# Last batch's C loaded in three parts, experts that pause behind each eviction, another order behind the loop

## The chip, the cores and the metric

One core of a Trainium2 chip runs the program. The metric is the device time of one execution in microseconds. TensorE is called PE here, VectorE DVE, ScalarE ACT, GpSimd POOL, and SyncE, which here only issues transfers, SP.

## What is computed

Eight batches of 3136 x 256 numbers go through a Fourier transform along the 3136 positions, a complex 256 x 256 weight with a soft threshold, and the inverse transform. Then, in each batch, the 128 positions with the highest score go through one expert (256 to 1024, ReLU, 1024 to 256), whose result is added with a sigmoid gate.

```python
X = np.fft.rfft(x, axis=1)
Yr = Xr @ w_r - Xi @ w_i + b_r
Yi = Xr @ w_i + Xi @ w_r + b_i
Yr = np.sign(Yr) * np.maximum(np.abs(Yr) - lam, 0.0)    # Yi likewise
y = np.fft.irfft(Y, n=x.shape[1], axis=1)
...
scores = np.einsum('bsd,d->bs', x, w_gate)
for b in range(B):
    top_idx = np.argpartition(-scores[b], capacity)[:capacity]
    xe = x[b, top_idx]
    ye = np.maximum(xe @ w1, 0.0) @ w2
    out[b, top_idx] = x[b, top_idx] + g[:, None] * ye   # g: sigmoid of the score
```

## The kernel before

**Stages.** The transform is factored as 98 x 32. Forward stage 1 (`s1`, lines 398 to 415) multiplies folded input by `w` and stores the result as `As` in DRAM. Forward stage 2 (`s2`, L441) reads `As` in units, 13 or 12 of them in each batch (the thirteenth of every second batch holds the odd rows of two batches). `spectral` (L223 to L225) multiplies a unit by the weights, `shrink` (L479, L481) thresholds it, `s2i` (L502) is inverse stage 2 and puts its result as `C` into DRAM (`Cs`), four units to a store (L525); it also reduces the score of each position on DVE (L514, `Csc`). `ld_c` reads C back in four blocks of 8 columns by 98 rows to a batch, 784 KB each; `s1i` (L570) is inverse stage 1 in eight pieces to a batch, and every second piece makes a group of three stores to the output.

**Experts.** `route` picks the positions of a batch: `score`, then `select`, which counts in eight rounds how many scores reach a threshold (one product, L243, and a string of DVE operations each; called a count below), then `place`, which makes the index `idx` (L326). `fetch` gathers the rows by an indirect transfer from POOL's queue (`xe`, L332). `ffn` takes an expert through `prepare` (transposes, L343, copy `xT`, L346, gate `ga` on ACT, L352), `hidden` (two halves of four pieces, L361, each half evicted with a ReLU to `hh`, L366) and `combine` (eight pieces, L372; `ye`, L377; scatter, L378). These are generators: each `yield` gives the turn back, and a `tick` runs them on to their next one.

**The order.** It is written out by hand: engines run what the program issues in the order in which it is issued. T = 100 steps, one per unit, each of which issues stage 2 of the next unit, the products of its own, inverse stage 2 of the unit before, and between them a piece or two of `s1` or `s1i`, the turns of `route`, and two or three ticks of the experts. SP's queue takes all large transfers in that order. `bank` names the PSUM bank of an expert's results; in the loop it is one bank, `m`, so the next results wait until the last are evicted.

**Behind the loop** a second loop goes on with t = T, T + 1, ... It issues the last unit's inverse stage 2, loads C of batch 7 (`rest` holds its eight pieces; `ready` says from which t a piece may be issued), and shares PE out between counts of batch 7, pieces of `s1i` and ticks of the experts, by an estimate of PE's time in `load`; `idle` issues products without use.

```python
    def ready():
        b, i = rest[0]
        return b < B - 1 or t > T + 4 + 3 * (i // 2) // 2
...
        for k in range(4):
            if t >= T and len(rest) <= (16, 16, 10, 8)[k] and (B - 1, k) not in cv:
                ld_c(B - 1, 2 * k)
                ld_c(B - 1, 2 * k + 1)
```

## Time and profile before

| | us |
|---|---|
| median of 3 runs | 728.84 (727.83 to 730.57) |
| the profiled execution | 729.37 |
| its span | 727.5 |
| PE busy | 650.9 (89%) |
| DVE busy | 443.8 (61%) |
| ACT busy | 364.6 (50%) |
| POOL busy | 293.5 (40%) |

The page gives these shares over the whole span. In the loop, from about 46 to 664 us, a step lasts between some 4.5 and 9 us, and PE's share is nine tenths or more in nearly every slice. Behind the loop the slices thin out. For the stretches between, the timeline of each engine, its list of waits and the chain that ended last are read: a wait in square brackets is the time that the engine sat idle before the row, and the releaser is what ended it.

### The profile page before, as it was taken

The numbers are of one execution on the slowest core, as the hardware profiler recorded it, in microseconds if no ns is written. First come the engines' busy times: TensorE is split into PE (matmuls) and PEld (weight loads), VectorE is DVE, ScalarE is ACT, GpSimd is POOL, SyncE is SP. The second block draws the span as 40 slices with busy tenths as digits, with TensorE's granted clock in tenths as the row PEclk, the third lists the DMA queues.
The fourth block names the chain that finished last, engine by engine and source line by source line (L and its number), as shares of the span: only waits on it lengthen the run. The fifth ranks groups of instructions, "written<-read, shape, count | busy, mean of one in ns | idle before, by whom it ended". The sixth has DMA issues, their size and how long they took to land.

```text
span 727.5 us, 20428 instructions
## 1 busy us (share of the span) xinstructions
PE 650.9 (89%) x8333; PEld 479.8 (66%) x8333; DVE 443.8 (61%) x1393; ACT 364.6 (50%) x671; POOL 293.5 (40%) x247
## 2 busy tenths in 40 slices
PE   2769989999999999999999999899999999987865
PEld 0247767767776677766777777676777777665535
DVE  4516566777677666656477566765676567773520
ACT  1326546466655565544555456555654555543230
POOL 4148565545445445345444445444542122221001
PEclk9869999999999999999999999999999999999996
DMA  8979976899989998979569778979785755754570
GB/s 150 277 233 318 264 205 166 221 300 263 276 259 272 308 292 236 312 217 269 177 166 296 216 220 223 326 228 249 224 256 158 208 161 156 235 169 113 189 171 23
DMA packets 79198, 163.73 MB, mean 225 GB/s; under 512 B 5918, under 2 KB 58496, under 8 KB 72832
## 3 DMA queue, kind: packets, MB, share of 16 engines
q1 hardware_dynamic: 77920, 160.15, 77.3%
q0 software_dynamic: 896, 2.17, 1.0%
q8 instruction: 66, 1.08, 0.6%
q14 instruction: 28, 0.23, 0.1%
q10 hardware_dynamic: 288, 0.10, 0.1%
HBM read 84.35 MB, written 78.12 MB: 223 GB/s over the span
## 4 chain that ended last, share of the span: by engine, by line
PE 59%; DVE 14%; DMA 12%; issue 6%; ACT 6%; POOL 2%; SPq 1%; POOLq 0%; DVEq 0%; ACTq 0%
PE pca L502 9%; PE s L570 6%; PE px L441 5%; DVE junk L514 5%; PE py L223 5%; PE py L225 4%; PE py L224 4%; PE s L407 4%; PE pcb L223 4%; PE m L361 3%; PE m L372 3%; DVE Xl L454 2%; ACT ct L512 2%; PE pcb L225 2%; PE pcb L224 2%
## 5 line engine op out<-in xcount | busy, mean ns | idle before, releaser
L470 POOL TENSOR_TENSOR kb<-ks,bias 128x512 f32<-128x512 f32 x100 | 127.9, 1279 | 323.6 <-ACT ks L468 322.0
L396 POOL TENSOR_TENSOR sd<-xt 113x512 f32<-113x512 f32 x106 | 133.8, 1284 | 28.4 <-DMA xt<-in_x 20.3
L512 ACT COPY ct<-pcb 128x256 f32<-128x256 f32 (+1 forms) x100 | 37.3, 373 | 170.5 <-PE pcb L502 159.8
L474 DVE TENSOR_TENSOR py<-py,kb 128x512 f32<-128x512 f32 x100 | 69.9, 699 | 78.9 <-POOL kb L470 73.9
L454 DVE TENSOR_TENSOR Xl<-px,Xh 128x768 fp32r<-128x768 f32 x100 | 95.6, 956 | 19.3 <-ACT Xh L453 19.3
L502 PE MATMUL pca<-Y,gi_sb 64*64 64x256 f32 x760 | 101.8, 386 | 5.8 <-DVE pca L240 5.5
L502 PE MATMUL pcb<-Y,gi_sb 64*64 64x256 f32 x768 | 103.3, 386 | 0.0
L514 DVE CUSTOM_DVE_ANT_0 junk<-pcb,wgb 128x256 f32<-128x256 f32 (+1 forms) x100 | 42.4, 424 | 98.9 <-ACT ct L512 97.4
L441 PEld LDWEIGHTS px<-g_sb,av 64*64 64x64 f32 x3072 | 78.9, 135 | 19.2 <-issue 5.7
L453 ACT CAST Xh<-px 128x768 fp32r<-128x768 f32 x100 | 81.0, 810 | 17.0 <-PE px L441 15.3
L441 PE MATMUL px<-g_sb,av 64*64 64x96 f32 x3072 | 84.3, 246 | 5.5 <-DMA av<-As 5.3
L407 PE MATMUL s<-sd,w 49*64 49x512 f32 x480 | 72.7, 638 | 12.9 <-DVE sd L396 10.7
L572 ACT COPY ot<-s 128x1024 f32<-128x1024 f32 x58 | 60.1, 1036 | 44.8 <-PE s L570 44.8
L479 ACT ACTIVATE r<-py,m2l 128x512 f32<-128x512 f32 x100 | 70.3, 703 | 8.2 <-DVE py L474 7.9
L502 PEld LDWEIGHTS pca<-Y,gi_sb 64*64 64x64 f32 x760 | 46.5, 132 | 41.9 <-issue 11.3
L409 ACT COPY at<-s 128x1024 f32<-128x1024 f32 x58 | 60.7, 1046 | 18.9 <-PE s L407 18.9
L481 DVE SCALAR_TENSOR_TENSOR Y<-py,r 128x512 f32<-128x512 f32 x100 | 68.5, 685 | 1.6 <-ACT r L479 1.6
L223 PE MATMUL pcb<-wsh,Xh 128*128 128x256 f32 x200 | 65.7, 328 | 1.2 <-DVE Csc L514 1.2
L570 PE MATMUL s<-cv,wi_sb 64*64 64x512 f32 x464 | 62.6, 599 | 0.0
L223 PE MATMUL py<-wnh,Xh 128*128 128x256 f32 x200 | 56.8, 284 | 1.3 <-DVE Y L481 1.2
L225 PE MATMUL pcb<-wsl,Xh 128*128 128x256 f32 x200 | 56.3, 281 | 0.0
L224 PE MATMUL pcb<-wsh,Xl 128*128 128x256 f32 x200 | 56.2, 281 | 0.0
(169 smaller groups left out, 1358.6 us busy)
## 6 DMA issues: line engine op xcount, KB each, us to landing
Cs<-ct SPq DMA_DIRECT2D x48, 512.0 KB
av<-As SPq DMA_DIRECT2D x46, 512.0 KB
As<-at SPq DMA_DIRECT2D x30, 784.0 KB
cv<-Cs SPq DMA_DIRECT2D x30, 784.0 KB
out<-ot SPq DMA_DIRECT2D x60, 384.0 KB
xt<-in_x SPq DMA_DIRECT2D x56, 384.0 KB
cv<-in_x SPq DMA_DIRECT2D x8, 384.0 KB
As<-ot SPq DMA_DIRECT2D x2, 784.0 KB
```

The lines of the kernel that those rows point to most:

```text
L223: nc.tensor.matmul(out, wh, mh, start=start, stop=False)
L224: nc.tensor.matmul(out, wl, mh, start=False, stop=False)
L225: return nc.tensor.matmul(out, wh, ml, start=False, stop=stop).ins
L396: eng.tensor_tensor(out=f[:113, k], in0=t[:113, 0], in1=t[:113, 1], op=op)
L407: nc.tensor.matmul(p[64 * c:64 * c + 64, r, :], w[64 * r:64 * r + NH, c, :], f[64 * r:64 * r + NH, c], start=True, stop=True)
L441: nc.tensor.matmul(o[:, :, N2 * j:N2 * j + N2], a[64 * p:64 * p + 64, j, g % 4, 128 * h + 64 * q:128 * h + 64 * q + 64], g_sb[64 * p:64 * ...
L453: nc.scalar.copy(out=vh, in_=v)
L454: nc.vector.tensor_tensor(out=vl, in0=v, in1=vh.bitcast(F32), op=ALU.subtract)
L470: nc.gpsimd.tensor_tensor(out=kb[:r], in0=ks[:r].broadcast_to([r, 2, D]), in1=bias[:r], op=ALU.add)
L502: nc.tensor.matmul(p[q][64 * a:64 * a + 64], gi_sb[64 * q:64 * q + 64, g, c, 64 * a:64 * a + 64], y[64 * q:64 * q + 64, c, :], start=(c == ...
L514: nc.vector.tensor_tensor_reduce(out=junk[:r], in0=p[k][:r], in1=wgb[:r], scale=1.0, scalar=0.0, op0=ALU.mult, op1=ALU.add, accum_out=Csc[ ...
L570: nc.tensor.matmul(p[64 * c:64 * c + 64, r, :], wi_sb[64 * r:64 + NH * r], f[64 * r:64 + NH * r, 4 * c + 2 * e:4 * c + 2 * e + 2, :], star ...
```

## The change

- C of batch 7 is loaded by `ld_last` instead of `ld_c`. Of each block, rows 0 to 31 and row 48 of both halves (66 of 98 rows) are the early part, rows 32 to 47 (32 rows) the late one. The early parts of blocks 0 and 1 are issued in step T - 2, that of block 2 in step T - 1, that of block 3 and the four late parts behind the last unit's store.
- `prepare` and each half of `hidden` are followed by `pause`, which gives turns back until the next step has begun, as long as the loop runs. The ReLU is issued right behind its half's last product, no longer with the next product.
- Behind the loop `ready` lets a piece of batch 7's `s1i` go from t > T + 2 + i // 2; the work in t = T is smaller (1.2, experts alone); batch 6's expert starts six steps behind its gather instead of three; eight idle products instead of six stand ahead of batch 7's expert.
- Batch 0's thirteenth unit and batch 1's first change places in the list of units.

```diff
--- before.py
+++ after.py
@@ -352,27 +352,37 @@
         nc.scalar.activation(out=ga, in_=sg, func=AF.Sigmoid)
         return xT, ga
 
+    def pause():
+        t = done["t"]
+        while done["t"] == t:
+            yield
+
     def hidden(b, k, xT, hs):
         n = min(128, cap - 128 * k)
         for q in range(FF // 512):
             ph = ps.tile([128, 4, n], F32, name=bank(b, 1 + q % 2), bufs=1)
             for f in range(4):
+                if f > 0:
+                    yield
                 for h in range(2):
                     nc.tensor.matmul(ph[:, f, :], w1s[:, h, (4 * q + f) * 128:(4 * q + f + 1) * 128], xT[:, h, :],
                                      start=(h == 0), stop=(h == 1))
                 load[0] += 0.45
-                yield
             hs.append(pool.tile([128, 4, n], F32, name="hh", bufs=2))
             nc.scalar.activation(out=hs[q], in_=ph, func=AF.Relu)
+            if done["t"] < T:
+                yield from pause()
+            else:
+                yield
 
     def combine(b, k, idx, xe, ga, hs):
         n = min(128, cap - 128 * k)
         py = ps.tile([n, D], F32, name=bank(b, 3), bufs=1)
         for f in range(FF // 128):
+            if f > 0:
+                yield
             nc.tensor.matmul(py, hs[f // 4][:, f % 4, :], w2s[:, f, :], start=(f == 0), stop=(f == FF // 128 - 1))
             load[0] += 0.43
-            if f < FF // 128 - 1:
-                yield
         ye = pool.tile([n, D], F32, name="ye", bufs=1)
         nc.vector.scalar_tensor_tensor(out=ye, in0=py, scalar=ga, in1=xe, op0=ALU.mult, op1=ALU.add)
         nc.gpsimd.indirect_dma_start(out=outs[b], out_offset=bass.IndirectOffsetOnAxis(ap=idx, axis=0),
@@ -551,13 +561,20 @@
             yield "db"
 
     def ld_c(b, i):
-        if i % 2:
-            return
-        k = i // 2
-        t = cv[b, k] = (xts if b == B - 1 and k < 2 else cvs)[k % 2]
-        if b == B - 1 and k < 2:
-            done["c7"] = done["t"]
-        ld(t[15:113], Cs[b].rearrange("r m n d -> (r m) n d")[:, 8 * k:8 * k + 8, :])
+        if i % 2 == 0:
+            cv[b, i // 2] = cvs[i // 2 % 2]
+            ld(cv[b, i // 2][15:113], Cs[b].rearrange("r m n d -> (r m) n d")[:, 4 * i:4 * i + 8, :])
+
+    def ld_last(k, early):
+        b = B - 1
+        if early:
+            cv[b, k] = (xts if k < 2 else cvs)[k % 2]
+        v = Cs[b][:, :, 8 * k:8 * k + 8, :]
+        for r in range(2):
+            a, n = (0, 32) if early else (32, 16)
+            ld(cv[b, k][15 + 49 * r + a:15 + 49 * r + a + n], v[r, a:a + n])
+        if early:
+            ld(cv[b, k][63:113:49], v[:, 48])
 
     def s1i(b, i):
         e = i % 2
@@ -605,6 +622,7 @@
     YB, XB, KB, RB, AB = 2, 2, 1, 1, 2
     G, U = 13, 8
     units = [u for b in range(0, B, 2) for u in [(b, g) for g in range(G)] + [(b + 1, g) for g in range(G - 1)]]
+    units.insert(13, units.pop(12))
     T = len(units)
     LEAD, LAG = 17, 18
     stores, spreads = [], []
@@ -639,7 +657,7 @@
                 while done["s1i"] < b or done["t"] < (40 if b < B - 3 else T - 4) or (b, k) not in slots or len(fetched) > 1:
                     yield
                 fetched.append((b, k, slots[b, k], gather(b, k, slots[b, k])))
-                age[b, k] = done["t"] + (2 if b < B - 2 else 3 if b < B - 1 else 0)
+                age[b, k] = done["t"] + (2 if b < B - 2 else 6 if b < B - 1 else 0)
                 yield
 
     def ffn():
@@ -648,9 +666,12 @@
                 yield
             item = fetched[0]
             if item[0] == B - 1:
-                idle(6)
+                idle(8)
             xT, ga = prepare(*item)
-            yield
+            if item[0] < B - 1:
+                yield from pause()
+            else:
+                yield
             hs = []
             yield from hidden(*item[:2], xT, hs)
             yield from combine(*item, ga, hs)
@@ -723,6 +744,9 @@
                 ld_a(*units[u])
         for b, i in loads[t] if t >= 0 else ():
             ld_c(b, i)
+        if t > T - 3:
+            for k in (0, 1) if t == T - 2 else (2,):
+                ld_last(k, True)
         if t in (0, 4, 8):
             consts_g(t // 4 + 1)
         if t in (-1, 1, 4, 9):
@@ -779,7 +803,7 @@
 
     def ready():
         b, i = rest[0]
-        return b < B - 1 or t > T + 4 + 3 * (i // 2) // 2
+        return b < B - 1 or t > T + 2 + i // 2
 
     def work(us, alone=False):
         turns = 0
@@ -804,11 +828,10 @@
             done["s2i"] = B - 1
             flush()
             load[0] = 0.0
-            work(1.4)
-        for k in range(4):
-            if t >= T and len(rest) <= (16, 16, 10, 8)[k] and (B - 1, k) not in cv:
-                ld_c(B - 1, 2 * k)
-                ld_c(B - 1, 2 * k + 1)
+            work(1.2, True)
+            ld_last(3, True)
+            for k in range(4):
+                ld_last(k, False)
         load[0] = 0.0
         turn("pe", "da", "db")
         us = 0.8 if t == T else 1.4 if t == T + 1 else 1.2 if t < T + 10 else 0.8
```

The first place is PE in step T - 2, at the transposes of batch 5's expert (L343). Before:

```order
L343 MATMUL m<-ident,xe 128x128 x2
L361 MATMUL m<-xT,w1s 128x128 x4
L502 MATMUL pca<-Y,gi_sb 64x256 x2
L502 MATMUL pcb<-Y,gi_sb 64x256 x2
L502 MATMUL pca<-Y,gi_sb 64x256 x2
L502 MATMUL pcb<-Y,gi_sb 64x256 x2
L289 LDWEIGHTS mt
L289 MATMUL pca<-tm,mt 98x64
L570 MATMUL s<-cv_85,wi_sb 64x512 x4
```

After (`L512` is `s2i`, `L587` is `s1i` there):

```order
L343 MATMUL m<-ident,xe 128x128 x2
L512 MATMUL pca<-Y,gi_sb 64x256 x2
L512 MATMUL pcb<-Y,gi_sb 64x256 x2
L512 MATMUL pca<-Y,gi_sb 64x256 x2
L512 MATMUL pcb<-Y,gi_sb 64x256 x2
L289 LDWEIGHTS mt
L289 MATMUL pca<-tm,mt 98x64
L587 MATMUL s<-cv_85,wi_sb 64x512 x4
```

The first four hidden products (L361) have left this step; inverse stage 2 follows the transposes directly.

The second place is PE behind the loop, from the first count of batch 7 (L243) on. `xt_82`, `xt_83`, `cv_84` and `cv_85` hold C's blocks 0 to 3. Before, with batch 5's expert ending (L372) and batch 6's beginning (L343):

```order
L243 MATMUL pca<-digits,n 128x15
L247 MATMUL pca<-ident,rep 98x8 x4
L372 MATMUL m<-w2s,hh 128x256 x2
L603 MATMUL pcb<-wsh 128x512
L243 MATMUL pca<-digits,n 128x15
L343 MATMUL m<-ident,xe 128x128 x2
L361 MATMUL py<-xT,w1s 128x128 x6
L243 MATMUL pca<-digits,n 128x15
L361 MATMUL py<-xT,w1s 128x128 x2
L361 MATMUL m<-xT,w1s 128x128 x4
L243 MATMUL pca<-digits,n 128x15
L570 MATMUL s<-xt_82,wi_sb 64x512 x4
```

After (`L384` is `combine`, `L587` is `s1i`):

```order
L243 MATMUL pca<-digits,n 128x15
L587 MATMUL s<-xt_82,wi_sb 64x512 x4
L384 MATMUL py<-w2s,hh 128x256
L243 MATMUL pca<-digits,n 128x15
L587 MATMUL px<-xt_82,wi_sb 64x512 x4
L384 MATMUL py<-w2s,hh 128x256
L243 MATMUL pca<-digits,n 128x15
L587 MATMUL s<-xt_83,wi_sb 64x512 x4
L587 MATMUL px<-xt_83,wi_sb 64x512 x4
L243 MATMUL pca<-digits,n 128x15
L587 MATMUL s<-cv_84,wi_sb 64x512 x4
L343 MATMUL m<-ident,xe 128x128 x2
```

The pieces of `s1i` begin behind the second count instead of the fourth, and batch 6's transposes have gone behind the fifth piece.

The third place is SP's queue around the last store of Cs. Before:

```order
L155 DMA out<-ot 96x1x1024 x2
L155 DMA out<-ot 2x2x1024
L525 DMA Cs_77<-ct 64x8x256 x2
L155 DMA xt_82<-Cs_77 98x2048
L155 DMA xt_83<-Cs_77 98x2048
L155 DMA cv_84<-Cs_77 98x2048
L155 DMA cv_85<-Cs_77 98x2048
```

After, beginning with the end of the early parts (block 0 and block 1's large ones stand ahead):

```order
L155 DMA xt_83<-Cs_77 2x2048
L155 DMA cv_84<-Cs_77 32x2048 x2
L155 DMA cv_84<-Cs_77 2x2048
L155 DMA out<-ot 96x1x1024 x2
L155 DMA out<-ot 2x2x1024
L535 DMA Cs_77<-ct 64x8x256 x2
L155 DMA cv_85<-Cs_77 32x2048 x2
L155 DMA cv_85<-Cs_77 2x2048
L155 DMA xt_82<-Cs_77 16x2048 x2
L155 DMA xt_83<-Cs_77 16x2048 x2
L155 DMA cv_84<-Cs_77 16x2048 x2
L155 DMA cv_85<-Cs_77 16x2048 x2
```

Early parts of three blocks now stand ahead of batch 6's last stores, and behind the store of Cs only 4 small pairs are left beside block 3's early part.

## Rows read from the trace of the kernel before

**Rows 1.** PE's waits, whole run: who waited, for whom; us in total, times, longest.

```profile
PE m L361 <- DVE xT L346: 5.0, 5, 1.4
...
PE pca L243 <- DVE Csc L514: 4.7, 4, 1.5
PE m L372 <- ACT hh L366: 3.9, 5, 1.2
PE pca L289 <- DVE Csc L514: 2.4, 2, 1.5
...
PE m L361 <- ACT hh L366: 1.9, 2, 1.2
...
PE m L343 <- DVE ye L377: 1.1, 1, 1.1
```

**Rows 2.** PE's timeline, step T - 2: start, us, names, [idle before].

```profile
653.88 1.16 PE L361 MATMUL m<-xT,w1s 128*128 128x128 f32 x8 [1.29 <-DVE xT L346]
```

**Rows 3.** PE's timeline behind the loop, same columns.

```profile
666.57 2.05 PE L361 MATMUL m<-xT,w1s 128*128 128x128 f32 x16 [1.25 <-ACT hh L366]
...
671.01 1.13 PE L372 MATMUL m<-w2s,hh 128*128 128x256 f32 x4 [1.18 <-ACT hh L366]
...
674.59 0.29 PE L243 MATMUL pca<-digits,n 128*128 128x15 f32 x2
...
677.19 0.39 PE L243 MATMUL pca<-digits,n 128*128 128x15 f32 x2 [0.73 <-DVE pca L240]
...
679.51 0.41 PE L343 MATMUL m<-ident,xe 128*128 128x128 f32 x2 [1.93 <-DMA xe<-out,idx]
...
692.82 0.31 PE L243 MATMUL pca<-digits,n 128*128 128x15 f32 x2
...
697.25 1.09 PE L570 MATMUL px<-cv,wi_sb 64*64 64x512 f32 x8
...
711.31 0.69 PE L343 MATMUL m<-ident,xe 128*128 128x128 f32 x2 [8.33 <-DMA xe<-out,idx]
...
712.61 3.75 PE L361 MATMUL s<-xT,w1s 128*128 128x128 f32 x16 [0.61 <-DVE xT L346]
...
719.07 3.62 PE L372 MATMUL px<-w2s,hh 128*128 128x256 f32 x16
```

**Rows 4.** PE's timeline: the first products of four steps in a row.

```profile
376.93 0.84 PE L441 MATMUL px<-g_sb,av 64*64 64x96 f32 x32
...
382.47 0.84 PE L441 MATMUL px<-g_sb,av 64*64 64x96 f32 x32
...
390.40 0.84 PE L441 MATMUL px<-g_sb,av 64*64 64x96 f32 x32
...
396.46 0.76 PE L441 MATMUL px<-g_sb,av 64*64 64x96 f32 x28
```

**Rows 5.** SP's queue behind the loop: start, us in which it issued, transfers.

```profile
671.00 0.75 SPq L155 DMA_DIRECT2D xt<-Cs  x2
...
689.48 7.29 SPq L155 DMA_DIRECT2D out<-at  x6
```

**Rows 6.** Stretches: length, busy us of PE, PEld, DVE, ACT, POOL; clock, DMA share, GB/s.

```profile
650.00:660.00 10.00, 7.17 (x66) 5.42 (x66) 5.12 (x21) 3.92 (x8) 1.28 (x1) 1.00 0.01 4
...
682.00:684.00 2.00, 2.00 (x12) 2.00 (x11) 0.70 (x4) 0.00 (x0) 0.00 (x0) 0.50 0.75 291
...
708.00:710.00 2.00, 0.00 (x0) 0.00 (x0) 0.00 (x0) 0.00 (x0) 1.25 (x2) 0.57 0.00 0
```

**Rows 7.** The page's costliest groups: busy us, mean ns of one, idle before.

```profile
L572 ACT COPY ot<-s 128x1024 f32<-128x1024 f32 x58 | 60.1, 1036 | 44.8 <-PE s L570 44.8
```

**Rows 8.** The chain that ended last: start, us, what.

```profile
702.25 5.24 DMA out<-ot
...
708.45 2.82 DMA xe<-out,idx
```

**Rows 9.** DVE's timeline behind the loop, columns as in rows 2.

```profile
700.95 0.15 DVE L326 TENSOR_TENSOR idx<-col,pca 128x1 uint32<-128x1 f32 x1
```

## The prediction

> **What bounds the kernel now.** I read four views in this order: the page's list of busy times, TensorE's (PE's) waits over the whole run, PE's timeline, and the chain that ended last. PE is busy 89% of the span (table above); in the loop it is the engine that everything waits for, so there a wait of PE's own is lost time, where the work behind it has slack. The list of waits shows the ones that the experts cause [rows 1]: their first product stands right behind the copy `xT` that it reads, the first product of the second half right behind the `hh` that empties its bank, and once a transpose behind `ye`. From about 664 us on the loop is over, and PE is no longer the bound: the end is a string of batch 7's C, its last inverse stage, its stores, one gather and one expert.
>
> I work the sum in the clock of the kernel before, as if the loop had gained nothing, and take the loop's part off at the end. The profiled execution took 729.37 us, 1.85 more than its span of 727.52; the median of the three runs is 728.84, 0.5 less.
>
> **Part 1: experts pause.** *Waits removed.* Over the run PE waited 5.0 us for `xT` in 5 places, of which 1.29 is step T - 2's [rows 2], so 3.7 in the loop; 3.9 for `hh` before the second product, 1.18 of it behind the loop [rows 3], so 2.7; 1.9 for `hh` before the first product, 1.25 of it behind the loop [rows 3], so 0.65; 1.1 for `ye` [rows 1]. Together 8.2 us. *New waits.* With a pause, PE comes to the next step's count earlier, but the count's bank is released by the score reductions on DVE, and these follow ACT's `ct` copies, which stand behind the expert's `ga` in ACT's queue. Such waits exist: 4.7 us in 4 [rows 1]. They are between 0 and 1.1 in each of the four steps that prepare an expert; I take 0.3, since a forward-stage product lies ahead of most counts, so -1.2. *Free room.* The step from 376.93 to 382.47 has no expert and lasts 5.54; the one from 390.40 to 396.46 has two hidden pieces (8 products; 1.03 us, half of the sixteen's 2.05 in [rows 3]) and lasts 6.06 [rows 4]. Half of that expert work was free. The pauses spread the same work into six steps that had none (by the order of the two kernels); six times 0.5 is 3.0. Half of those steps carry other extra work, for which no such row stands, so I take 2.0 of 0 to 3.0. The step from 382.47 to 390.40, which prepares and goes straight on, lasts 7.93 [rows 4]: that is what a pause breaks up. *Step T - 2* loses the wait of 1.29 and moves 1.16 us of products behind the loop [rows 2]: between 1.2 and 2.45, less what ACT keeps by `ga`; I take 1.7. Sum of part 1: 8.2 - 1.2 + 2.0 + 1.7 = **10.7 us** (5 to 13.7).
>
> The exchanged units (batch 0's last unit one step later, batch 1's first one earlier) move the same products by a step; their loads stay two or three steps ahead on SP's queue. I cost that at nothing; the cover is that lead, and without it one load's wait, of the size of the 1.1 us in [rows 1], would show.
>
> **Part 2: the tail.** *C.* Before, all 3.1 MB of batch 7's C are issued at 671.00, when the last Cs store has landed [rows 5], and batch 6's gather lies in the same transfers: PE waits 1.93 for `xe` [rows 3]. Now C blocks 0 to 2 (rows 0 to 31 and row 48) go out in the last two steps. The DMA engines move almost nothing there (share 0.01 from 650 to 660 [rows 6]), which hides them. On SP's queue they stand ahead of batch 6's last stores and the last Cs store; nine issues of about 0.4 us (two took 0.75 [rows 5]) are done long before those. After the store there remain the early part of block 3 and 1 MB of late rows, eight issues, 3 us at the same rate. My estimate, with 1 to 2 us from issue to landing and the 291 GB/s of [rows 6]: the first block is whole at 673.5, the last at 677.
>
> *Counts.* Half of the two waits of 1.25 and 1.18 stays (the second half's first product still needs the bank), so the first count is at 672.9 instead of 674.59; the second 2.6 later as before [rows 3], at 675.5. Then PE goes count, piece of the inverse stage, piece of expert. A piece of the inverse is 1.03 (its row of 1.09 overlaps its neighbours), an expert's 0.45 to 0.51 (3.62 / 8 and 2.05 / 4), a count 0.25 (0.31 in its row, overlapped): about 1.75 a round [rows 3]. Six rounds are 10.5, one has two inverse pieces (+0.6), and DVE takes `ye` and `xT` in between (+0.2): 11.3. The eighth count is at 686.8, against 692.82: 6.0 earlier.
>
> *Stores.* The first two inverse pieces end at 678.45, ACT's copy takes 1.04 [rows 7], so the first store goes at 679.5 instead of 689.48 [rows 5]; the eighth piece is at 687.1 instead of 697.25 [rows 3]. From first issue to last landing it took 702.25 + 5.24 - 689.48 = 18.0 us [rows 5, 8]. The pieces come as fast as before or faster, so transfers set this; I keep 18.0: landed at 697.5. The index of batch 7, written at 700.95 before [rows 9], follows the eighth count and is there at 695.1: not last. The gather starts 0.96 after the landing and takes 2.82 [rows 8]: `xe` at 701.3 instead of 711.3: **10.0 us** (7 to 11).
>
> *Last expert.* [...] At the full level both halves and the transposes would save 2.6 of 11.4 us. Now batch 6's expert and eight idle products end at about 698, which leaves PE idle some 3 us. A gap like that cuts both ways in the rows: after 703 the clock held for 5 us (a mean of 0.57 over 2 us is 0.3 us at the full level), but after the wait of 1.93 at 677.6 to 679.5 it was at half from 682 to 684 [rows 3, 6]. I take half, 1.3. [...]
>
> Sum of part 2: 10.0 + 1.3 = **11.3 us** (7 to 13.6).
>
> **Sum.** 729.37 - 10.7 - 11.3 = 707.4 against the profiled execution, 706.9 against the median: 707.
>
> **Rivals.**
> (a) The clock falls in the last gap as before. For it: [rows 6]; against: a gap of 3 instead of 8 us. 708.2. Chance 0.16.
> (b) Late C in front of the counts. An inverse piece of batch 7 now stands directly behind the second count, in PE's one order, so if its rows come late every count behind waits too. Before, C needed until 684 (DMA still at 291 GB/s from 682 to 684 [rows 6]); if the late rows came then, 8 us of the tail are lost: 715. Against it: a third of the bytes. Chance 0.11.
> (c) The experts' waits only change their name: PE runs into the score reductions instead. Part 1 shrinks to about 2: 716. For it: the waits of 4.7 and 2.4 us for `Csc` [rows 1]. Chance 0.13.
> (d) Slower. Every `hh` and `ga` is now put into ACT's queue in the step of its products, ahead of `ct`, and PE's next count waits for what follows `ct`. There are 16 such pauses in the loop. At the longest wait of this kind, 1.5 us [rows 1], they cost 24 and eat the whole gain; from 1.7 each the kernel is slower by more than 0.5%, 733. Against it: PE issues that step's inverse products meanwhile, so `ct` has to wait for those in any case. Chance 0.04.
>
> **How the numbers follow.** The forecast, 702 to 712, has 0.56. The range goes from the best ends of the two sums (13.7 and 13.6, 701.6) up to case (b): 701 to 715; it leaves out (c), (d) and little else. About 0.5% is what a measurement of this kernel can tell from no change. All cases but (d) are faster by more; (d) or (b) and (c) together give the rest: faster 0.95, same 0.02, slower 0.03.
>
> **What would show it.** In the profile of the changed kernel: PE's waits for `xT`, `hh` and `ye` gone in the loop, and its last step's end some 9 to 12 us earlier; if waits for `Csc` grew by as much, (c). The early C loads in a stretch where DMA is idle, and the eight late ones landed before the first inverse piece of batch 7; PE waiting there for a DMA means (b). Less than 12 us between second and eighth count. The gather of batch 7 directly behind the last store's landing, some 10 us earlier against the loop's end. Sixteen products of the last expert in 2.05 or 3.75 us decide (a). The forecast is wrong if the stores take longer than 18 us because they start in a crowd, or if the index comes last.

## The result, and the profile after

The changed kernel takes 707.63 us (median of 4 runs, 705.88 to 711.43), the kernel before beside it 729.06 (727.83 to 730.57): a ratio of 0.971, 95% interval 0.967 to 0.976. The forecast was 707 (701 to 715). In a second comparison the changed kernel took 706.65 (700.40 to 713.16) and the kernel before 734.47; ratio 0.961 (0.955 to 0.966). Ratios leave out single executions that were disturbed.

The profiled execution of the changed kernel is the longest of its first four: 711.43 us, span 709.7. Its loop gained a little more than forecast, its tail less; the shorter executions make up for that. Three marks on PE cut the run into stretches: the first product of step 42 (just ahead of the experts of the loop), the first product of the last step's stage 2 (called step 99 below), and the first product of the last unit's inverse stage 2. The first two, of before and then of after (start, us, names):

```profile
278.63 0.59 PE L441 MATMUL px<-g_sb,av 64*64 64x96 f32 x20
...
648.14 0.56 PE L441 MATMUL px<-g_sb,av 64*64 64x96 f32 x16
```

```profile
279.90 0.34 PE L451 MATMUL px<-g_sb,av 64*64 64x96 f32 x7
...
637.22 0.48 PE L451 MATMUL px<-g_sb,av 64*64 64x96 f32 x12
...
652.36 0.65 PE L512 MATMUL px<-Y,gi_sb 64*64 64x256 f32 x4 [0.26 <-DVE Y L491]
```

Before, the third mark stood at 663.90. So the stretch from step 42 to step 99 shrank from 369.5 to 357.3 us; at the last inverse stage 2 the gain is 11.5 us; from there to the end of the span it went from 63.6 to 57.3.

PE's waits in that stretch of the loop, before and then after (who waited, for whom; us in total, times, longest):

```profile
PE pca L243 <- DVE Csc L514: 3.8, 3, 1.5
PE m L361 <- DVE xT L346: 3.7, 4, 1.4
PE pca L502 <- DVE pca L240: 2.9, 10, 0.3
PE m L372 <- ACT hh L366: 2.8, 4, 0.7
...
PE m L343 <- DVE ye L377: 1.1, 1, 1.1
...
PE pca L531 <- DVE Csc L514: 0.7, 1, 0.7
PE m L361 <- ACT hh L366: 0.7, 1, 0.7
```

```profile
PE pca L243 <- DVE Csc L524: 3.4, 4, 1.5
PE pca L512 <- DVE pca L240: 2.5, 9, 0.3
PE m L343 <- DMA xe<-out,idx: 1.1, 1, 1.1
PE s L417 <- ACT ot L589: 0.9, 2, 0.5
```

The waits of [rows 1] for `xT`, `hh` and `ye` have left the loop. Those for `Csc` did not grow in their place in this trace (6.3 us before, 5.2 after; 6.6 in the second trace of the changed kernel); a small one for `ot` is new.

The tail, PE's timeline (rows that answer to [rows 3]):

```profile
661.28 0.29 PE L243 MATMUL pca<-digits,n 128*128 128x15 f32 x2
...
664.20 1.08 PE L587 MATMUL s<-xt,wi_sb 64*64 64x512 f32 x4
665.81 1.79 PE L587 MATMUL s<-xt,wi_sb 49*64 49x512 f32 x4 [0.54 <-DMA xt<-Cs]
...
668.91 1.99 PE L587 MATMUL px<-xt,wi_sb 64*64 64x512 f32 x8
...
682.00 0.29 PE L243 MATMUL pca<-digits,n 128*128 128x15 f32 x2
...
694.99 0.41 PE L343 MATMUL m<-ident,xe 128*128 128x128 f32 x2 [1.73 <-DMA xe<-out,idx]
695.91 3.04 PE L368 MATMUL s<-xT,w1s 128*128 128x128 f32 x16 [0.52 <-DVE xT L346]
```

And stretches of it (length, busy us of PE, PEld, DVE, ACT, POOL; granted clock, DMA share, GB/s):

```profile
660.00:664.00 4.00, 3.48 (x19) 2.78 (x20) 2.24 (x12) 0.42 (x1) 0.23 (x1) 1.00 1.08 191
664.00:668.00 4.00, 3.46 (x11) 1.03 (x12) 1.37 (x7) 0.36 (x1) 0.00 (x0) 0.76 0.98 139
668.00:672.00 4.00, 4.00 (x16) 1.99 (x15) 1.37 (x7) 1.66 (x2) 0.00 (x0) 0.50 0.17 25
672.00:676.00 4.00, 4.00 (x20) 1.14 (x18) 1.76 (x8) 1.03 (x2) 1.00 (x1) 0.50 0.65 141
```

The first count is where it was forecast: 661.28 + 11.5 = 672.8 in the clock of before, forecast 672.9. The first inverse piece then waits inside itself for late rows of C, and behind that wait the granted clock goes to 0.50 until 676: whole pieces take 1.99 us instead of 1.09. The eighth count comes 18.1 us behind the second, where 11.3 were forecast. Note the DMA column: engines busy all the time (0.98 to 1.08), yet 139 to 191 GB/s.

### The profile page after: what moved, and what is told of

The parts are those of the page before. It is cut to its first block, busy times and chain, and to the rows that moved or that the text cites. A ratio compares the mean times of both kernels' runs of the same rounds, so it can differ in the third digit from the quotient of the medians.

```text
span 709.7 us, 20460 instructions
## 1 busy us (share of the span) xinstructions
PE 651.6 (92%) x8334; PEld 479.1 (68%) x8334; DVE 443.3 (62%) x1393; ACT 364.7 (51%) x671; POOL 293.4 (41%) x247
## 3 DMA queue, kind: packets, MB, share of 16 engines
q8 instruction: 66, 1.08, 0.6%
## 4 chain that ended last, share of the span: by engine, by line
PE 59%; DVE 14%; DMA 14%; issue 5%; ACT 4%; POOL 2%; SPq 1%; POOLq 0%; DVEq 0%; ACTq 0%
PE pca L512 9%; PE s L587 6%; DVE junk L524 5%; PE py L223 5%; PE px L451 5%; PE py L224 4%; PE py L225 4%; PE s L417 4%; PE pcb L223 4%; PE m L368 3%; DMA As<-at 3%; PE m L384 2%; PE pcb L225 2%; PE pcb L224 2%; DVE Xl L464 2%
## 5 line engine op out<-in xcount | busy, mean ns | idle before, releaser
L512 PE MATMUL pca<-Y,gi_sb 64*64 64x256 f32 x760 | 101.8, 386 | 5.6 <-DVE pca L240 4.7
L512 PE MATMUL pcb<-Y,gi_sb 64*64 64x256 f32 x768 | 102.9, 386 | 0.0
L463 ACT CAST Xh<-px 128x768 fp32r<-128x768 f32 x100 | 81.1, 811 | 17.6 <-PE px L451 15.0
L512 PEld LDWEIGHTS pca<-Y,gi_sb 64*64 64x64 f32 x760 | 46.4, 132 | 41.3 <-DVE pca L240 11.4
L419 ACT COPY at<-s 128x1024 f32<-128x1024 f32 x58 | 60.7, 1046 | 18.5 <-PE s L417 18.4
L587 PE MATMUL s<-cv,wi_sb 64*64 64x512 f32 x464 | 61.9, 602 | 0.0
L243 PEld LDWEIGHTS pca<-digits,n 128*128 128x128 f32 x128 | 20.0, 194 | 54.1 <-DVE Csc L524 50.5
```

The lines of the kernel that those rows point to most:

```text
L463: nc.scalar.copy(out=vh, in_=v)
L512: nc.tensor.matmul(p[q][64 * a:64 * a + 64], gi_sb[64 * q:64 * q + 64, g, c, 64 * a:64 * a + 64], y[64 * q:64 * q + 64, c, :], start=(c == ...
L587: nc.tensor.matmul(p[64 * c:64 * c + 64, r, :], wi_sb[64 * r:64 + NH * r], f[64 * r:64 + NH * r, 4 * c + 2 * e:4 * c + 2 * e + 2, :], star ...
```

## The experiments

Times are medians (lowest to highest); ratios are against the kernel before in the same comparison, whose median was 734.47, 732.47 and 732.56 us in the three. That is 3 to 5 us more than in the first one, so ratios and traces are compared rather than medians of different comparisons. The changed kernel itself gave 0.971 in the first and 0.961 in the second: a difference of 0.01 between runs of different comparisons shows nothing by itself. From each profiled execution, in us:

| kernel | median (range) | ratio (95%) | to step 42 | 42 to 99 | 99 to last inverse stage 2 | from there to the end |
|---|---|---|---|---|---|---|
| before | 729.06 | 1 | 278.6 | 369.5 | 15.8 | 63.6 |
| changed | 707.63 (705.9–711.4) | 0.971 (.967–.976) | 279.9 | 357.3 | 15.1 | 57.3 |
| changed, again | 706.65 (700.4–713.2) | 0.961 (.955–.966) | 279.5 | 357.7 | 15.5 | 53.3 |
| pauses alone | 716.91 (714.0–720.5) | 0.977 (.972–.982) | 282.4 | 357.0 | 16.7 | 61.5 |
| pause behind `prepare` alone | 724.14 (722.2–725.3) | 0.988 (.982–.994) | 281.5 | 364.4 | 13.9 | 60.8 |
| tail alone | 721.29 (717.5–727.9) | 0.986 (.980–.992) | 279.9 | 370.2 | 15.8 | 51.4 |
| units back | 708.12 (705.5–716.1) | 0.968 (.962–.973) | 280.3 | 357.9 | 15.2 | 50.2 |
| C whole | 707.12 (703.4–714.7) | 0.965 (.960–.970) | 284.9 | 356.9 | 16.7 | 54.5 |
| late C by half | 715.08 (712.7–716.3) | 0.975 (.971–.980) | 278.2 | 359.7 | 15.1 | 61.2 |
| two blocks whole | 706.42 (703.4–708.7) | 0.964 (.959–.968) | 283.7 | 356.7 | 15.5 | 50.3 |
| 16 idle products | 708.83 (706.6–716.4) | 0.970 (.964–.976) | 282.9 | 356.9 | 15.5 | 50.4 |
| pieces in pairs | 708.16 (703.5–714.7) | 0.964 (.958–.970) | 282.0 | 358.0 | 15.1 | 51.2 |
| old `ready` | 709.79 (703.1–711.8) | 0.966 (.961–.972) | 282.0 | 356.6 | 16.7 | 54.7 |
| old `age` | 711.40 (707.0–718.9) | 0.970 (.964–.975) | 282.1 | 357.1 | 16.6 | 61.3 |

### The changed kernel again

> The changed kernel itself once more, beside the other three, for their comparison and for a second trace: 706 to 709 us. If the tail of its first profiled execution (711 us) was a late landing of C's last rows followed by a fall of the clock, and its shorter executions have neither, a trace of a shorter execution has no stretch at half clock between 666 and 676 us, its second-to-eighth count takes 11 to 13 us instead of 18, and the tail is 4 to 5 us shorter. Rival: the tail is the same in all executions, and the difference lies elsewhere (in the loop, or behind the stores).

In this trace the tail is 4.0 us shorter, and no row between 664 and 692 us runs at half clock:

```profile
664.22 0.39 PE L243 MATMUL pca<-digits,n 128*128 128x15 f32 x2 [0.52 <-DVE pca L240]
664.54 2.21 PE L587 MATMUL s<-xt,wi_sb 64*64 64x512 f32 x8
...
677.38 0.29 PE L243 MATMUL pca<-digits,n 128*128 128x15 f32 x2
...
691.29 0.41 PE L343 MATMUL m<-ident,xe 128*128 128x128 f32 x2 [2.67 <-DMA xe<-out,idx]
```

The first piece takes 2.21 instead of 1.09, so the wait for late C of 1.1 us is there as well; the clock holds, and the eighth count comes 13.2 us behind the second. The loop is equal within 0.4 us. What sets the two tails apart is whether the clock falls behind that wait; why it fell in one execution and held in the other stays open.

### Units in their old order

```diff
-    units.insert(13, units.pop(12))
```

> The changed kernel with the list of units in its old order. The prediction cost the exchange at nothing: the same time as the changed kernel within 0.3%, 706 to 709 us. Rival from the two traces: the changed kernel's step 36 has a wait for `at`<-`As` of 1.3 us that the kernel before hasn't; if the exchange makes it, this kernel is 1.3 us faster than the changed one, 706.3, and the wait is gone from its trace. Second rival, the exchange gains something where the trace hides it: 1 to 2 us slower, 709.

The interval lies beside that of the changed kernel (0.961) with an overlap, and the trace shows the loop within 0.6 us. The suspected wait for `at` in step 36 is there without the exchange too (1.0 us here, 1.3 and 0.7 in the two traces with it). No cost of the exchange can be seen, and this trace has the shortest tail of all with the changed order, 50.2 us.

### Pauses alone, and one of them

The kernel before with the changed `hidden` and `combine`, `pause`, and this in `ffn`:

```diff
             xT, ga = prepare(*item)
-            yield
+            if item[0] < B - 1:
+                yield from pause()
+            else:
+                yield
```

> The kernel before with the pauses alone: `prepare` and both halves of `hidden` give turns back until the next step, the ReLU stands behind its half's last product; loads of C, `ready`, the shares of work behind the loop and the list of units are those of before. My theory: the loop's part of the gain stands by itself, 10.7 us (by the steps of the two traces 10 to 11.5 at the last unit's inverse stage 2), and the tail is as long as before: 718 to 719 us, ratio 0.984 to 0.987. Rival, the waits only change their name: a gain of about 2, 727 us. Rival, the tail gives part of it back, since work that the loop no longer holds stands behind it: a gain of 7 to 9, 720 to 722.

The same with the pause behind `prepare` only (in `hidden`):

```diff
-            if done["t"] < T:
-                yield from pause()
-            else:
-                yield
+            yield
```

> The kernel before with the pause behind `prepare` alone; both halves of `hidden` go straight on as before, the tail is that of before. Between step 42 and the last step's stage 2, PE took 369.5 us before and 357 with all pauses (three traces within 1 us). By the prediction's sum the four waits for `xT` there (3.7 us) and some of the free room go, the waits for `hh` (3.4 us) and for `ye` (1.1) stay: 364 to 365.5 us for that stretch, and with step T - 2 some 5 to 6 us of the whole. Rival: the free room is the larger part, so that breaking up the longest step is nearly all: 359 to 361. Second rival: only with the halves in steps of their own is there any gain: 367 or more.

All pauses: the stretch from step 42 to 99 takes 357.0 us, 12.6 less than before, and the tail 61.5, 2.1 less; so nothing is given back behind the loop. (The span gained only 10.0 in that trace, since the steps ahead of 42 took 3.8 us longer; see the last section.) The pause behind `prepare` alone gives 364.4, 5.1 less, within what was expected. Its waits:

```profile
PE pca L243 <- DVE Csc L521: 5.4, 6, 1.5
PE m L368 <- ACT hh L372: 3.4, 5, 0.7
```

`xT` is gone, `hh` stands as it did, and `ye` went with `xT`, which was not expected. All waits for `Csc` together grew from 6.3 to 8.0 us here. So this pause carries 5.1 of the 12.6 us; the rest comes with the pauses behind the halves, which were not run without it. The rival "waits only change their name" falls: the pauses alone gain 2.3%, where it had 0.3%.

### Tail alone

The changed kernel with `hidden` and `combine` of before, and in `ffn`:

```diff
-            if item[0] < B - 1:
-                yield from pause()
-            else:
-                yield
+            yield
```

> The changed kernel without the pauses: `hidden`, `combine` and the turn behind `prepare` as before; the three-part loads of C, the order behind the loop and the exchanged units as changed. My theory by the sum of the prediction: 11.3 us less than before, 717.5. By the profiled execution of the changed kernel, in which C's last rows came late and the clock fell at 666 us: 6 to 7 us less, 722. Rival, the two parts lean on each other (the early C rows collide with the experts' work that pauses had moved): 4 us less or nothing, 725 to 729. If both parts are worth what they are worth together, the gains of this run and of the pauses alone add up to 21 to 22 us.

Ratio 0.986, about 10 to 13 us. Its loop takes 370.2 (before 369.5), its tail 51.4 instead of 63.6: 12.2 us. The two parts add: 0.977 x 0.986 = 0.963, the changed kernel beside them had 0.961.

### How C is loaded

Whole blocks behind the last store, at once; PE's order is that of the changed kernel:

```diff
-        if t > T - 3:
-            for k in (0, 1) if t == T - 2 else (2,):
-                ld_last(k, True)
...
-            ld_last(3, True)
             for k in range(4):
-                ld_last(k, False)
+                cv[B - 1, k] = (xts if k < 2 else cvs)[k % 2]
+                ld(cv[B - 1, k][15:113], Cs[B - 1].rearrange("r m n d -> (r m) n d")[:, 8 * k:8 * k + 8, :])
```

> The changed kernel with batch 7's C loaded whole (four transfers of 98 rows, 784 KB each) behind the last store of Cs, none of it earlier; PE's order is the changed kernel's to the instruction. The prediction's step was that early C makes the early inverse pieces possible: then the first piece waits for a block that comes later, and the tail is 3 to 5 us longer, 710 to 712. Rival from the two traces: in the changed kernel, the late 16-row transfers move only about 140 GB/s (8 KB packets of 0.9 us, all DMA engines busy), so that the last of C lands some 13 us after the store was issued, just as late as the whole 3.1 MB did before at 290 GB/s; then loading it whole costs nothing, 705 to 708, the first piece's second half waits 0 to 1 us as it does now, and the gain of the tail belongs to the order on PE alone.

Late rows of all first halves, then of all second halves:

```diff
-            for k in range(4):
-                ld_last(k, False)
+            b = B - 1
+            for r in range(2):
+                for k in range(4):
+                    ld(cv[b, k][47 + 49 * r:63 + 49 * r], Cs[b][r, 32:48, 8 * k:8 * k + 8, :])
```

> The changed kernel with its eight late C transfers in another order on SP's queue: first the 16 rows of the first half of all four blocks, then those of the second half (now the two halves of a block alternate). Theory: the low rate comes from the few partitions that a transfer writes, 16 in one place; with four transfers in a row onto the same 16, packets of 8 KB take longer than the 0.9 us of now, 1.1 to 1.8, the first piece's second half waits 3 us or more, and the kernel takes 709 to 713 us. Rival: the rate is set by something that does not depend on the place (a cost for each transfer, or the reading of rows just written): packets stay at 0.9 us; the first piece then waits only for the four transfers that now stand ahead of its second half, 2 to 3 us more, 708 to 710. The packet times tell the two apart.

Blocks 0 and 1 in parts, late rows first; blocks 2 and 3 whole:

```diff
-        if t > T - 3:
-            for k in (0, 1) if t == T - 2 else (2,):
+        if t == T - 2:
+            for k in range(2):
                 ld_last(k, True)
...
-            ld_last(3, True)
-            for k in range(4):
+            for k in range(2):
                 ld_last(k, False)
+            for k in range(2, 4):
+                cv[B - 1, k] = cvs[k % 2]
+                ld(cv[B - 1, k][15:113], Cs[B - 1].rearrange("r m n d -> (r m) n d")[:, 8 * k:8 * k + 8, :])
```

> The changed kernel with blocks 0 and 1 of batch 7's C in two parts as now and blocks 2 and 3 whole behind the last store: the late rows of blocks 0 and 1 come first on SP's queue, seven small transfers fewer stand there. By the rates of the traces, late rows of two blocks 0.5 MB at 140 GB/s and two whole blocks 1.6 MB at 290: 9 us, where now 10; block 0 whole 2 to 3 us earlier than now. Theory: the first piece of the inverse no longer waits (1.1 us in it now), counts and stores come 1 us earlier: 705 to 706 us. Rival: the tail's bound is the store string and batch 6's expert, the piece's wait is made up for later: no change, 706 to 708.

The first of these overturns a step of the prediction: loading C whole costs nothing that can be measured (707.12, ratio 0.965 against 0.961, intervals overlapping). Its profiled execution is its longest (714.7), with the clock at half from about 672 to 679 (0.58 and 0.57 over the two stretches of 4 us from 672 on); even so, the first piece waits only this long:

```profile
671.20 1.09 PE L587 MATMUL s<-xt,wi_sb 64*64 64x512 f32 x8 [0.79 <-DMA xt<-Cs]
```

The first block is whole 12.7 us behind the last inverse stage 2 here, and 13.5 us behind it in the first trace of the changed kernel: early C brings it no sooner, since the small transfers moved 135 GB/s and the whole blocks of the kernel before 299. Rows by stretch, of the kernel before (98-row transfers, 674 to 676), the changed one (16 rows, the two halves of a block by turns, 664 to 666), and the one with late rows by half (16 rows, four transfers in a row onto the same partitions, 668 to 670):

```profile
674.00:676.00 2.00, 2.00 (x15) 1.80 (x13) 0.88 (x7) 0.00 (x0) 0.00 (x0) 1.00 0.96 299
```

```profile
664.00:666.00 2.00, 1.46 (x8) 0.56 (x10) 1.37 (x7) 0.00 (x0) 0.00 (x0) 1.00 0.96 135
```

```profile
668.00:670.00 2.00, 0.48 (x2) 0.29 (x4) 0.00 (x0) 0.00 (x0) 0.00 (x0) 0.50 1.05 111
```

The DMA engines are equally busy and move 299, 135 and 111 GB/s. By the records of single packets, the median one of 8 KB took 0.42, 0.91 and 1.20 us in these stretches. So the theory of place came out as expected: with the same bytes and the same transfers, only their order changed, packets got slower. PE waited, in part also because block 0's second half now stands behind four transfers:

```profile
669.52 1.97 PE L587 MATMUL s<-xt,wi_sb 49*64 49x512 f32 x4 [3.60 <-DMA xt<-Cs]
```

Within that wait of 3.6 us the clock goes to half (0.50) and stays there to 684, and the kernel is 6 to 9 us slower than the other three of this comparison, more than expected. The order changes which rows of DRAM are read one after the other as well; no run separates that from the place that is written.

With two blocks whole, the late rows of blocks 0 and 1 come first on the queue. The same view shows both speeds side by side, and the first piece has no wait at all:

```profile
666.00:668.00 2.00, 1.48 (x10) 0.91 (x13) 1.39 (x7) 0.00 (x0) 0.00 (x0) 1.00 0.84 156
668.00:671.00 3.00, 3.00 (x21) 1.09 (x14) 2.29 (x12) 1.16 (x2) 0.00 (x0) 1.00 0.93 300
```

```profile
667.70 1.09 PE L587 MATMUL s<-xt,wi_sb 64*64 64x512 f32 x8
```

Its tail is 50.3 us, and its executions lie closer together (703.4 to 708.7) than the changed kernel's (700.4 to 713.2), but the median is that of the changed kernel within the spread.

### The order behind the loop

```diff
-        return b < B - 1 or t > T + 2 + i // 2
+        return b < B - 1 or t > T + 4 + 3 * (i // 2) // 2
```

> The changed kernel with the old rule for the inverse pieces of batch 7 (from t > T + 4 + 3 (i // 2) // 2): the first stands behind the fourth count again, the rest as changed, early C too. Theory: the tail's gain is the place of the pieces, since the string of stores begins with the second of them: stores 6 us later, 712 to 714 us. Rival: the stores' start is not what sets the end, the experts' order and the early C carry it: 706 to 709.

```diff
-                age[b, k] = done["t"] + (2 if b < B - 2 else 6 if b < B - 1 else 0)
+                age[b, k] = done["t"] + (2 if b < B - 2 else 3 if b < B - 1 else 0)
```

> The changed kernel with batch 6's expert three steps behind its gather again instead of six, the pieces where the changed kernel has them. Its transposes then stand behind the third piece, and the last pieces come two rounds later, among the products of the index. Theory: the last pieces, and with them the stores' end, come 2 to 4 us later: 709 to 711. Rival: the stores have slack there, no change: 706 to 707.5.

Two blocks whole, and in three rounds two pieces:

```diff
+        if T + 3 < t < T + 7:
+            for i in range(2):
+                s1i(*rest.pop(0))
+                load[0] += 1.0
         work(us, t < T + 2)
```

> The kernel with blocks 2 and 3 of C whole, and two inverse pieces in each of three rounds behind the loop (before, one in a round, but for one of two): the last piece ends 10.5 us behind the second count instead of 13.5, and batch 6's expert begins a round later. Theory: PE's inverse pieces set the string of stores as much as the transfers do, so stores end 2 to 3 us earlier; the index of batch 7, which follows the eighth count (0.5 to 1 us later now), then comes last in front of the gather, about 1.5 to 2 us earlier than the landing of the stores now: 704 to 705 us. Rival: the transfers alone set the string's end (3.2 MB in 18 us from its first to its last, whatever comes first), and it begins where it began: no change, 706.5. Second rival, ACT's copies (1.04 us each, two in a round of 2.3 us) hold the pieces up: no change or slower.

With the old `ready`, about half of the expected loss came: 709.79, 3 us above the changed kernel's second comparison, and the intervals overlap. In its trace the first store is issued 18.9 us behind the last inverse stage 2, against 16.2 to 17.1 in the three traces with pauses and the changed kernel's C and `ready` in which the clock held up to there. It is 2 to 3 us later and not 6, because two counts without pieces now follow each other quickly, and two pieces stand behind the fourth:

```profile
666.81 0.39 PE L243 MATMUL pca<-digits,n 128*128 128x15 f32 x2 [0.52 <-DVE pca L240]
668.80 0.39 PE L243 MATMUL pca<-digits,n 128*128 128x15 f32 x2 [0.41 <-DVE pca L240]
670.80 0.39 PE L243 MATMUL pca<-digits,n 128*128 128x15 f32 x2 [0.36 <-DVE pca L240]
671.12 1.09 PE L587 MATMUL s<-xt,wi_sb 64*64 64x512 f32 x8
```

Before, 7.9 us lay between the second and the fourth count (677.19 [rows 3] and 685.07), here 4.0: batch 6's transposes and their wait for `xe` no longer stand between them. That is the work of `age`. With the old `age` the median is 711.40; the profiled execution is its longest and ran at half clock from 669 to 697 (0.50 in every stretch from 672 to 696), so places are not read from it. The medians put each of the two edits at some 2 to 5 us, but 0.966 and 0.970 lie between the two ratios of the changed kernel itself, so neither loss is shown clear of the spread.

The pairs bring no gain: 708.16. The last piece ends 3.4 us earlier against the loop's end than with two blocks whole, but the gather only 0.9 us (33.6 instead of 34.4 us behind the last inverse stage 2):

```profile
671.09 6.14 SPq L155 DMA_DIRECT2D out<-at  x6
677.34 7.53 SPq L155 DMA_DIRECT2D out<-ot  x6
...
688.59 0.48 DVE L387 SCALAR_TENSOR_TENSOR ye<-py,ga,xe 128x256 f32<-128x256 f32 x1 [1.45 <-PE py L384]
688.65 0.97 POOL L332 DMA_INDIRECT xe<-out,idx  x1 [9.53 <-PE py L384]
```

From the first store to the gather it is 17.6 us with the pieces early, 18.4 with them as they were: the first rival, the transfers set the string. The releaser that the row names misleads. By the trace's records the last store landed at 687.74, 0.91 us ahead of the gather; in all other traces but one the gather comes 0.88 to 0.96 us behind that landing, whatever its row names, and here it starts before batch 6's `ye` has ended. In the chain that ended last of the changed kernel's second trace the store stands by its name, landing at 687.51 in front of a gather at 688.38:

```profile
682.34 5.17 DMA out<-ot
```

The one exception is the tail alone, at 1.10 us: there the index, at 698.58, came 0.2 us behind the last landing. So little more is to be had from faster stores. No version tried beats the changed kernel by what can be measured.

### More idle products

```diff
-                idle(8)
+                idle(16)
```

> The changed kernel with sixteen idle products instead of eight ahead of batch 7's expert: PE's gap before it shrinks from 1.1 to 2.7 us (in three traces) to about 0, as eight products take 2.2 us. Theory: where the clock falls in that gap, the first half's sixteen products take 3.0 to 3.3 us instead of 2.05, so that the clock costs 1.0 to 1.6 us in some executions and nothing in others; now it never falls there: 0.5 to 1 us faster than the changed kernel, and its first half is 2.05 in the trace. Rival: the sixteen products themselves come last (the transposes wait behind them): 0.5 to 1 us slower.

```profile
688.24 4.00 PE L620 MATMUL pcb<-wsh 128*128 128x512 f32 x16
692.68 0.41 PE L343 MATMUL m<-ident,xe 128*128 128x128 f32 x2 [0.43 <-DMA xe<-out,idx]
693.60 2.05 PE L368 MATMUL s<-xT,w1s 128*128 128x128 f32 x16 [0.52 <-DVE xT L346]
```

In the trace it does what was expected: a gap of 0.43, sixteen products in 2.05 us. Three traces with eight idle products have the 2.05 as well. The median (708.83) shows no gain; what it is worth, at most 1.6 us in the executions in which the clock would fall, is below the spread.

## Why the prediction held, step by step

**Part 1, forecast 10.7, measured 11.5 at the last inverse stage 2.** It is 12.2 us from step 42 to 99, 0.6 in the next stretch, and 1.3 lost ahead of step 42, where the pauses do not act and other traces lie between 278 and 285.
- *Waits removed*, 8.2: the rows above give 3.7 + 3.5 + 1.1 = 8.3. Right.
- *New waits*, -1.2: not seen. The waits for `Csc` went from 6.3 to 5.2 us in the first trace and 6.6 in the second; the new ones for `ot` are 0.9 and 1.0. With smaller changes the net is about +1 in the first and +0.3 in the second. With the pause behind `prepare` alone they did grow, by 1.7.
- *Free room*, 2.0 of 0 to 3.0: the lists of waits add up to 19.0 and 9.7, so 9.3 of the 12.2 us are waits, and the 2.9 left over are put down to room (the granted clock is 1.00 over this stretch in both). That is what remains, not a row of its own; it lies at the upper end of the bounds.
- *Step T - 2*, 1.7: mis-sized. The products moved and the wait for `xT` went, but `ct`, whose products now end earlier, has to wait for `ga` ahead of it in ACT's queue, as rival (d) had it: `ct` starts at 643.39 although its products end at 642.68, and PE waits 2.15 where it waited 1.53. Behind that wait the granted clock falls until about 649 (0.64 from 645 to 647, 0.51 from 647 to 649):

```profile
644.83 0.19 PE L289 MATMUL pca<-tm,mt 64*98 64x64 bf16 x1 [2.15 <-DVE Csc L524]
```

```profile
645.00:647.00 2.00, 2.00 (x13) 0.83 (x13) 1.03 (x8) 0.53 (x1) 0.00 (x0) 0.64 0.93 209
647.00:649.00 2.00, 2.00 (x12) 2.00 (x11) 0.59 (x4) 0.85 (x2) 0.33 (x1) 0.51 0.16 43
```

It fell behind that wait in ten of the eleven traces that have all pauses. With the pause behind `prepare` alone the wait is as long (2.12) and the clock held (1.00 from 651 to 659), and the stretch took 13.9 us: there the 1.7 came (1.9). So the clock took the gain, not the wait. In four of the ten it also fell behind a wait of 1.54 us for `Csc` at the count just ahead of this stretch (0.50 from 640 to 642 with the pauses alone), which stood in the kernel before too (1.53) without a fall; in these four the stretch takes 16.6 to 16.7 us, longer than before.
- *Exchanged units*, 0: their run shows nothing against it.

**Part 2, forecast 11.3.** Measured 6.3 in the first trace, 10.3 in the second, 12.2 to 13.4 in five others in which the clock held through counts and pieces (tail alone, units back, two blocks whole, 16 idle products, pairs). The forecast lies between.
- *C*: the step that failed. The first block was forecast whole at 673.5 (clock of before), and its late rows came at 677.3: the second of its two late transfers, issued at 660.02, took 5.74 us to land. The forecast had 1 to 2 us from issue to landing beside the rate; by the records of the trace of before, the loads of `w` and `wi_sb` at its start took 1.8 and 2.1. The term at fault is the 291 GB/s of [rows 6], taken for transfers of 16 rows that move 135; their issue took 4.6 us on SP's queue where 3 were forecast; and they stood behind block 3's early part, while the run that put them first has no wait. And early C was not needed: whole blocks, all loaded at the end, feed the pieces as well. So the gain of the tail belongs to what is left of the change there, the order on PE; how it divides between `ready`, `age` and the smaller edits is not shown.
- *Counts*: first and second right to 0.1 us. Second to eighth, 11.3: with the clock held 13.2, and 12.1 once the late C was out of the way; 18.1 with it fallen. The round of 1.75 us was too short: it took 1.99 (669.37 to 671.36 with two blocks whole), and as long in the rows of the old `ready` above, where PE has only short work between counts and waits 0.41 and 0.36 us for DVE (666.81 to 668.80 and 670.80). There DVE's string of a count sets the round, not PE's sum.
- *Stores*: the first went at 683.5 in the first trace and at 680.8 in the second (clock of before), forecast 679.5. From there 18.0 and 0.96 more to the gather, 19.0: it took 17.2 to 18.8 us where the clock held, 20.0 in the first trace. The reading that transfers set it was right; the pairs show it.
- *Gather*: 2.73 to 2.85 us. The index was there 3 us ahead of the gather (685.3 against 688.4 in the second trace). Right. Against the loop's end the gather came 4.9 us earlier in the first trace, 8.9 in the second and 10.3 with the units back, forecast 10.0.
- *Last expert's clock*, 1.3: from the transposes to the end it took 14.7 us in both traces of the changed kernel, before 16.2: 1.5 saved. Right as half. The prediction had put the whole at 2.6, half of which is the 1.3; no run shows that 2.6: where the clock held (1.00 from 692 to 704 with two blocks whole) it took 13.0, 3.2 saved.

**The rivals.** (a) happens in some executions: the sixteen products took 3.0 to 3.7 us in seven of eleven traces with a changed tail and 2.05 in four. The length of the gap alone did not decide: behind a gap of 1.25 us the clock fell (pieces in pairs, sixteen products in 3.68), behind one of 2.38 it held (two blocks whole, 1.00 from 692 to 700). No run shows what does. (b) came true in part, by another cause than the count of bytes: 0.5 to 1.1 us of waiting, and in the first trace 10 us at half clock behind it. (c) and (d) fell as totals; (d)'s mechanism acts in step T - 2 alone.

So the sum was right to 1 us while some of its terms were not: new waits and room came out 3 us better than taken, and step T - 2, the time ahead of step 42 and, in some executions, the late rows of C took that back. That these errors cancel to 1 us is luck; the two mechanisms, waits behind evictions in the loop and the order on PE behind it, are borne out by the pauses alone and the tail alone. The gain, forecast as 22 us, was 21 in the first comparison and 28 in the second, in which the kernel before took 5 us longer; no trace of it was taken there, so why stays open.

## What to carry to other kernels

Where an engine waits right behind each eviction, moving the next use to the following step can remove the wait, if other work fills the step (8.3 us of waits here); price that by the list of waits, and look for room that comes with it (2.9 us were left over here). Ask of an early load whether the late remainder moves at the same rate: here a third of the bytes took more than half the time of all (some 8 us against 12). After a short wait, read the clock column of the next rows: waits of about 1 us cost 3 us in step 37 and 4 to 5 in the tail where the clock fell behind them. And check a releaser that a row names against the rows of the other traces.

## What had not been expected of the hardware

- Transfers of 16 rows were slow here while DMA looked as busy: 299 GB/s for 98 rows (DMA share 0.96), 135 for 16 by turns in two places (0.96), 111 for 16 in one place (1.05).
- In the first trace of the changed kernel the clock fell behind two waits of 0.52 and 0.54 us close together (around 664 us; 0.51 from 666 to 668); in the second it held behind 0.52 and 1.1 us (whole pieces in 1.09).
- A part of the spread between executions lies ahead of the experts: two waits of about 1 us for `at` in steps 36 and 37, present with and without the exchange. Where the clock falls behind them, step 37 takes 10.4 us instead of 7.5, as here with two blocks whole:

```profile
250.38 0.54 PE L459 MATMUL px<-gt_sb,at 64*64 64x192 f32 x4 [0.98 <-DMA at<-As]
251.82 0.74 PE L459 MATMUL px<-gt_sb,at 64*64 64x192 f32 x10 [0.89 <-DMA at<-As]
```

```profile
250.00:254.00 4.00, 2.72 (x24) 1.20 (x24) 1.60 (x6) 1.51 (x3) 1.22 (x1) 0.80 1.07 335
254.00:258.00 4.00, 4.00 (x18) 3.40 (x17) 0.96 (x2) 1.39 (x2) 1.09 (x1) 0.50 0.97 299
```
